# A spectral mixing layer and a feed-forward layer on one core: the first filter piece cast with its neighbours, and the work around it moved

## The chip, the cores and the metric

The kernel runs on one core of a Trainium2 chip. The time is the device time of one execution in microseconds, and lower is better. Times within the profiled execution are counted from the start of its span. PE is TensorE (matrix products, with PEld for its weight loads), DVE is VectorE, ACT is ScalarE, POOL is GpSimd, SP is SyncE. SP and POOL issue the DMAs here: SP's go over a hardware queue, POOL's over a software queue, and only POOL's cast or accumulate on the way.

## What is computed

The input `x` holds 8 images of 3008 rows and 256 channels. Each image is filtered in the frequency domain, and the rows then pass through two matrix products with a PReLU between them.

```python
X = np.fft.rfft(x, axis=1)                        # x: 8 x 3008 x 256
F = (filt_r + 1j * filt_i)[None, :, :]            # 1505 x 256
y = np.fft.irfft(X * F, n=3008, axis=1)
h = y.reshape(24064, 256) @ w_in                  # 256 x 2048
g = np.maximum(h, 0.0) + alpha * np.minimum(h, 0.0)
out = g @ w_out                                   # 2048 x 256, float32
```

## The kernel before

The transform length is split as 3008 = 94 x 32, so that the transform of an image becomes small matrix products with constant tables: a first product over 94 points (`piece_a`), a turn of the axes, a second product over 32 points with the twiddle factors in the table `twf` (`piece_b`), the product with the filter, an inverse product with `twi` (`piece_c`), a turn back, and a last product over the 94 frequencies (`inverse`, called from `half_d` and `pair_d`), which writes `yT`, the filtered image with channels on the partitions. `yT` holds two images.

**Image 0** is handled by the class `First`, ahead of everything else (lines 359 to 449), with the turns done on PE through an identity matrix. Its second stage has 12 pieces `kp`. For each, `piece_b` makes a product on PE (L299), and DVE multiplies it with the filter into `uu` (L304). Then `piece_c` (L324) makes the inverse product into two banks `self.ops` and `keep_c` evicts them into `v`, two pieces at a time. The loop at lines 412 to 434 runs `piece_b` two pieces ahead of `piece_c`. `piece_c` takes its banks from the pool `psO`, which has two, for pieces 0 to 10, and from `psF`, which has one double bank, for piece 11. The pool `psH` has two double banks, written `hps`. `warm` (L376) issues products of the identity whose results nobody reads. After the loop, `half_t` turns `v` into `zt` (L346), and `half_d` makes the first quarter of `yT`.

The **filter** arrives in `filt_s`, cast to FP16 by POOL's DMAs in batches of pieces 1 to 3, 4 to 7 and 8 to 11, eight DMAs each (L122). Piece 0 is loaded by SP in FP32 into the tile `fst` and multiplied from there. `fst` has the tag `asb`, so it shares its buffer with `asb`, the first-product result of images 1 to 7. After the loop POOL copies `fst` into piece 0 of `filt_s` (L435), and then makes `filts_s`, the filter with its real and imaginary halves exchanged (L438, L440), for the later images.

The **tables** `twf`, `twi` and `twx` are loaded by SP in thirds (L365). A small DVE memset on the destination holds an SP or POOL DMA back until DVE has come that far: before the `fst` loads at i == 1, before the middle third of `twf` and the tables behind it at i == 3, before the later `twi` and `twx` thirds after `piece_b(0)`, and before the weights at kp == 4. ACT doubles each `twf` third into `twd` (`twice`). SP and POOL work through their DMAs in the order of the program, each waits for its own conditions, and whatever stands behind it waits too. The DMAs of a queue share eight semaphores in turn, so that one waits until the one eight places before it has landed.

**The matrix products** of the feed-forward layer run in 48 blocks of 512 (in places 384) rows. A block has 16 steps; in step j, `up(j)` makes the 128 hidden channels j with `w_in` (L485), ACT evicts two steps' worth into `gtb` (L494), DVE applies the slopes (L497, L499), and `down(j)` makes a sixteenth of the block before with `w_out` (L516). ACT evicts its result and SP stores it. `al_s` and `alm_s`, the slopes on the partitions, come from a PE transpose of `al16` (L447).

**Images 1 to 7** are worked on between those steps. `plan_fft` puts each piece at a step number, counted through all blocks; the order by engine is the order of the program, and nothing reorders it. For image 1, `piece_b` and its accumulating DMA `uu<-ww` on POOL (L191) stand at steps 36 to 66, `piece_c` (L210) at `c_at`, and the `pair_d` pieces at `d_at`, which write `yT` through the one `psF` bank; the second image's rows are first read at step 96. `x_at` are the steps at which POOL loads the next image's `xs`. Steps listed as `front` (those of `piece_a` and `piece_c`) run `down` ahead of the piece.

Of the kernel before, what the change touches and what calls it, by code (L numbers as in the profile page):

```python
# [10 lines left out]
FP32 = mybir.dt.float32  # L11
# [39 lines left out]
def kernel(  # L51
# [211 lines left out]
    class First(Fft):  # L263
        def __init__(self):
            super().__init__(0)
            self.at = p_fft.tile([128, NK, D], FP16, name="at")
            self.v = p_fft.tile([128, NK, D], FP16, name="v")
            self.zt = p_fft.tile([96, N2, D], FP16, name="zt")
            self.fst = p_fft.tile([128, 1, 2, D], FP32, name="fst", tag="asb")
            self.twd = gtb[:, 6:9].rearrange("p a b c -> p (a b c)").rearrange("p (k m) -> p k m", m=128)  # L270
            self.am = gtb[:, 0:6].rearrange("p a b c -> p (a b c)")
            self.vm = self.v.rearrange("p k d -> p (k d)")
# [20 lines left out]
        def piece_b(self, kp):  # L293
            hp = psH.tile([128, 2, 512], FP32, name="hps").rearrange("p r (i d) -> p r i d", i=2)
            for i in range(2):
                for par in range(2):
                    r = slice(64 * par, 64 * par + 64)
                    for e in range(2):
                        nc.tensor.matmul(hp[64 * e : 64 * e + 64, par, i],  # L299
                                         self.twd[r, 2 * kp + e, 64 * i : 64 * i + 64], self.at[r, 2 * kp + e],  # L300
                                         start=True, stop=True)
            uu = p_uw.tile([128, 2, 2, D], FP16, name="uu", bufs=3)
            fl = self.fst if kp < 1 else filt_s
            nc.vector.tensor_mul(uu, hp, fl[:, kp].unsqueeze(2).to_broadcast([128, 2, 2, D]))  # L304
            self.uw[kp] = uu

        def piece_c(self, kp):
            if kp % 2 == 0:
                self.ops = [psO.tile([128, 2, D], FP32, name="op") for _ in range(2)]
            if kp == 11:  # L310
                pf = banks(False)
                warm(2, pf[:, 0])
                self.ops = [pf[:, e].rearrange("p (k d) -> p k d", k=2) for e in range(2)]
            kb = 0 if kp == 11 else kp % 2
            u = self.uw.pop(kp)
# [53 lines left out]
    tables(nc.sync, ("twf",), 0, 8)  # L369
    load_filt(nc.gpsimd, filt_s, 1, 4)  # L370
    load_filt(nc.gpsimd, filt_s, 4, 8)
    load_filt(nc.gpsimd, filt_s, 8, 12)

    def warm(n, pw):
# [5 lines left out]
    for i in range(8):  # L380
        f0.piece_a(i, both[i % 2], i % 3 < 2)
        if i % 2 == 1:
            warm((4, 4, 6, 3)[i // 2], bank("o"))
        if i == 1:
            nc.vector.memset(f0.fst[:, 0, :, 0:1], 0.0)
            load_filt(nc.sync, f0.fst, 0, 1)
        if i == 3:
            nc.vector.memset(twf_s[:, 8:16, 0:1], 0.0)
            tables(nc.sync, ("twf",), 8, 16)
            tables(nc.sync, ("twi", "twx"), 0, 8)  # L390
            tables(nc.sync, ("twf",), 16, 24)
        if i == 5:
            f0.twice(0, 8)
# [18 lines left out]
    for kp in range(12):  # L412
# [5 lines left out]
        elif kp % 2 == 1:  # L418
            f0.keep_c(kp - 1, (on_act, on_act))
            if kp < 7:  # L420
                f0.turn_at(kp + 5, 2, on_act)
        if kp == 4:
            nc.vector.memset(win_s[:, 0, 0:2], 0.0)
            for kt in range(2):
                nc.gpsimd.dma_start(out=win_s[:, kt], in_=moe_w_in[kt * 128 : (kt + 1) * 128])
            xc[(1, 0)] = load_x(1, 0)
            for q in range(2):
                nc.gpsimd.dma_start(
                    out=wout_s[:, 8 * q : 8 * q + 8],
                    in_=moe_w_out[1024 * q : 1024 * q + 1024].rearrange("(j p) d -> p j d", p=128))  # L430
            for c in range(1, 4):
                xc[(1, c)] = load_x(1, c)
        if 7 <= kp < 10:
            warm(2, banks(False)[:, 0])
    nc.gpsimd.dma_start(out=filt_s[:, 0:1], in_=f0.fst)  # L435
    for o in range(0, 128, 64):
# [7 lines left out]
    for i, evict, kind, fill in ((0, on_act, "h", 1), (2, on_dve, "o", 0), (1, on_act, "o", 1), (3, on_dve, "f", 0)):  # L444
        f0.half_d(i, evict, kind, fill)
    alp = bank("o")
    nc.tensor.transpose(alp[:, 0:16], al16, id32)  # L447
    nc.vector.tensor_copy(al_s, alp[:, 0:16])
    nc.vector.tensor_scalar(alm_s, al_s, 1.0, -1.0, OP.mult, OP.add)

# [79 lines left out]
    def plan_fft(b, a_at, ta, quarters, x_at, b_at, add, c_at, d_at):  # L530
# [99 lines left out]
```

## Time and profile before

| what | value |
| --- | --- |
| median of 3 runs | 785.22 us (784.51 to 788.92) |
| profiled execution | 786.87 us |
| its span | 784.8 us |
| PE busy | 768.7 us (98%) |
| DVE, ACT, POOL busy | 595.2, 587.3, 142.6 us |
| chain that ended last, by engine | PE 92%, DMA 3%, DVE 2%, ACT 2% |
| end of the last filter product of image 0 | 32.75 us |
| first product of the feed-forward layer | 39.33 us |

The profile is a table of all instructions of one execution. A row gives the start and the length in us, the engine, the line of the kernel, the operation with output and input, the count of merged instructions, and in brackets how long the engine had been idle before it and what the trace takes to have ended that idle time. The last is an inference; where several things are waited for, the trace names one of them. A row of a window gives a stretch of time, and for each engine its busy time and its instructions, then the granted PE clock as a share of full speed, the DMA share and the GB/s.

### The profile page before, as it was taken

Reading aid. Unit: us, or ns where it says so; the run is one execution under the profiler, and the core shown is the slowest. Engines: PE = TensorE matmul, PEld = TensorE weight load, DVE = VectorE, ACT = ScalarE, POOL = GpSimd, SP = SyncE. Lnnn points to the kernel's source line nnn. Section 1 sums busy time; section 2 is a strip of 40 time slices with the busy share of each in tenths; the row PEclk is TensorE's granted clock in tenths of the full one; section 3 lists DMA queues with packets and bytes.
Section 4 is the critical chain, followed back from the end, with each engine's and each line's share of the span. In section 5 each row is a group of like instructions: output and inputs, shape, how many; then the busy total and the mean of one; then the engine's idle time right before and its main releaser. Section 6 shows DMA issues by size and latency. Waiting matters only on the chain.

```text
span 784.8 us, 16091 instructions
## 1 busy us (share of the span) xinstructions
PE 768.7 (98%) x6349; PEld 511.6 (65%) x6349; DVE 595.2 (76%) x1117; ACT 587.3 (75%) x673; POOL 142.6 (18%) x271
## 2 busy tenths in 40 slices
PE   8889999999999999999999999999999999999998
PEld 4546656666666666766666666766666666766666
DVE  3757985788868888788877888688877888766664
ACT  4678778888778877798767887788876777677664
POOL 6510571122102220122201222010210122000000
PEclk9999999999999999999999999999999999999999
DMA  9996697757754657555593655734474233511111
GB/s 174 163 183 187 129 204 173 221 135 166 142 153 108 147 135 148 135 127 122 132 206 82 146 127 128 189 81 108 110 153 129 57 86 92 145 40 28 42 41 54
DMA packets 95515, 100.64 MB, mean 128 GB/s; under 512 B 11328, under 2 KB 83280, under 8 KB 95248
## 3 DMA queue, kind: packets, MB, share of 16 engines
q1 hardware_dynamic: 80800, 70.25, 34.3%
q0 software_dynamic: 14640, 29.38, 21.6%
q8 instruction: 49, 0.80, 0.4%
q14 instruction: 26, 0.21, 0.1%
HBM read 55.28 MB, written 46.66 MB: 130 GB/s over the span
## 4 chain that ended last, share of the span: by engine, by line
PE 92%; DMA 3%; DVE 2%; ACT 2%; issue 1%; POOL 0%; SPq 0%; ACTq 0%; DVEq 0%; POOLq 0%
PE hps L485 41%; PE op L516 41%; PE hps L155 3%; PE psF L232 3%; PE psF L179 2%; PE hps L210 1%; DMA uu<-ww 1%; DMA twf_s<-c_twf 1%; ACT v L255 1%; ACT gtb L494 1%; DMA xs<-in_x_dram 1%; PE psF L346 1%; DMA fst<-in_filt_r_dram 1%; DVE m L497 1%; PE op L324 0%
## 5 line engine op out<-in xcount | busy, mean ns | idle before, releaser
L494 ACT ACTIVATE gtb<-hps 128x1024 f16<-128x1024 f32 (+1 forms) x384 | 385.8, 1005 | 133.1 <-PE hps L485 132.2
L516 PE MATMUL op<-wout_s,gtb 128*128 128x256 f16 x3008 | 436.3, 273 | 0.1
L485 PE MATMUL hps<-yT,win_s 128*128 128x512 f16 (+1 forms) x1536 | 434.9, 375 | 1.2 <-ACT gtb L494 1.1
L516 PEld LDWEIGHTS <-gtb 128*128 128x128 f16 x3008 | 294.0, 98 | 168.9 <-issue 0.9
L497 DVE TENSOR_SCALAR m<-gtb,alm_s 128x512 f16<-128x512 f16 (+1 forms) x768 | 232.8, 346 | 152.5 <-ACT gtb L494 151.5
L499 DVE TENSOR_TENSOR gtb<-gtb,m 128x2048 f16<-128x2048 f16 (+1 forms) x192 | 231.0, 1203 | 10.1
L485 PEld LDWEIGHTS <-win_s 128*128 128x128 f16 x1536 | 142.8, 98 | 61.4 <-issue 15.2
L193 POOL DMA_DIRECT2D sw<-ww x144 | 71.0, 501 | 380.8 <-DVE ww L186 377.9
L255 ACT ACTIVATE asb<-hps 96x1024 f16<-96x1024 f32 x56 | 57.1, 1020 | 13.9 <-PE hps L155 12.0
L521 ACT ACTIVATE osb<-op 128x512 f32<-128x512 f32 (+1 forms) x97 | 56.2, 579 | 5.3 <-issue 2.8
L255 ACT ACTIVATE v<-hps 128x1024 f16<-128x1024 f32 x42 | 43.0, 1025 | 15.9 <-PE hps L210 15.9
L255 ACT ACTIVATE yT<-psF 128x752 f16<-128x752 f32 x59 | 47.0, 797 | 7.8 <-PE psF L232 7.7
L112 POOL DMA_DIRECT2D xs<-in_x_dram x64 | 37.3, 672 | 82.6 <-PE hps L155 74.3
L186 DVE TENSOR_TENSOR ww<-psF,filts_s 128x1024 f16<-128x1024 f32 x42 | 51.1, 1217 | 0.0
L187 DVE TENSOR_TENSOR uu<-psF,filt_s 128x1024 f16<-128x1024 f32 x42 | 51.0, 1214 | 0.0
L155 PE MATMUL hps<-xs,wf_s 94*96 94x512 f16 x112 | 33.9, 384 | 2.0 <-ACT asb L255 2.0
L232 PE MATMUL psF<-wi_s,zt 96*128 96x94 f16 x500 | 31.2, 205 | 0.2
L232 PEld LDWEIGHTS <-zt 96*128 96x128 f16 x512 | 28.6, 98 | 2.9 <-issue 0.6
L191 POOL DMA_DIRECT2D uu<-ww x24 | 19.4, 1198 | 31.7 <-DVE uu L187 28.5
L198 DVE TENSOR_TENSOR uu<-uu,sw 128x1024 f16<-128x1024 f16 x36 | 24.6, 683 | 0.0
L210 PE MATMUL hps<-uu,twi_s 64*64 64x256 f16 x336 | 16.8, 271 | 1.5 <-DMA uu<-ww 0.8
L179 PE MATMUL psF<-at,twf_s 64*64 64x256 f16 x336 | 17.3, 281 | 0.0
(68 smaller groups left out, 171.6 us busy)
## 6 DMA issues: line engine op xcount, KB each, us to landing
out_dram<-osb SPq DMA_DIRECT2D x160, 128.0 KB
a_dram<-asb SPq DMA_DIRECT2D x28, 384.0 KB
v_dram<-v SPq DMA_DIRECT2D x84, 128.0 KB
zt<-v_dram SPq DMA_DIRECT2D x28, 384.0 KB
sw<-ww POOLq DMA_DIRECT2D x144, 64.0 KB, 2.3
at<-a_dram SPq DMA_DIRECT2D x20, 384.0 KB
xs<-in_x_dram POOLq DMA_DIRECT2D x32, 192.0 KB, 4.6
xs<-in_x_dram POOLq DMA_DIRECT2D x32, 184.0 KB, 5.9
```

What stands on the lines that cost most here:

```text
L155: nc.tensor.matmul(ps[0:96, u], wf1_s, xs[:, o : o + 512], start=True, stop=True)
L186: nc.vector.tensor_mul(ww, px, fs)
L187: nc.vector.tensor_mul(uu, px, f)
L193: nc.gpsimd.dma_start(out=sw[o : o + 32], in_=ww[i : i + 32])
L232: nc.tensor.matmul(ps[:, m], self.zt[:, 8 * g + 4 * mh + m, dh * 128 : dh * 128 + 128], wi3_s, start=True, stop=True)
L255: nc.scalar.activation(o, i, AF.Copy)
L485: nc.tensor.matmul(self.hps[:, j % 2, 0:tn], win_s[:, kt, j * 128 : (j + 1) * 128], yT[:, kt, self.t0 : self.t0 + tn], start=(kt == 0), st ...
L494: nc.scalar.activation(g[:, 2 * i : 2 * i + 2], self.hps[:, :, 0:tn], AF.Copy)
L497: nc.vector.tensor_scalar(m[:, 2 * i + h], g[:, 2 * i + h], 0.0, a, OP.min, OP.mult)
L499: nc.vector.tensor_add(g, g, m)
L516: nc.tensor.matmul(self.op[:, si - s0], self.gts[k][:, 128 * si : 128 * si + 128], wout_s[:, k], start=(si == s0 and k == 0), stop=(si == ...
L521: nc.scalar.activation(osb[:, 0:m], self.op[:, 0:m], AF.Copy)
```

## The change

The tile `fst` goes. Piece 0 of the filter is cast by POOL in one batch with pieces 1 to 3, and its copy into `filt_s` and the memset for it go. The weights and the loads of image 1 stand directly behind the filter on POOL's queue, with no memset to hold them. The tables that were issued at i == 3 are issued at i == 5. Piece 10 of the inverse takes its two banks from `psF`, and piece 11 takes one from `psH` and one from `psO`; the two fill products ahead of piece 11 write to the `psH` bank. The transpose of the slopes moves from ahead of the blocks to step 1. In the plan, image 1's `piece_c` moves from steps 48 to 78 to steps 50 to 80, four of its `pair_d` pieces and one `xs` load move by one or two steps, and the first six of image 2's `piece_a` steps move two steps earlier.

```diff
-            self.fst = p_fft.tile([128, 1, 2, D], FP32, name="fst", tag="asb")
...
-            fl = self.fst if kp < 1 else filt_s
-            nc.vector.tensor_mul(uu, hp, fl[:, kp].unsqueeze(2).to_broadcast([128, 2, 2, D]))
+            nc.vector.tensor_mul(uu, hp, filt_s[:, kp].unsqueeze(2).to_broadcast([128, 2, 2, D]))
...
-            if kp % 2 == 0:
+            if kp % 2 == 0 and kp < 10:
                 self.ops = [psO.tile([128, 2, D], FP32, name="op") for _ in range(2)]
+            if kp == 10:
+                pf = banks(False)
+                self.ops = [pf[:, e].rearrange("p (k d) -> p k d", k=2) for e in range(2)]
             if kp == 11:
-                pf = banks(False)
-                warm(2, pf[:, 0])
-                self.ops = [pf[:, e].rearrange("p (k d) -> p k d", k=2) for e in range(2)]
-            kb = 0 if kp == 11 else kp % 2
+                pf = [bank(kind) for kind in ("h", "o")]
+                warm(2, pf[0])
+                self.ops = [t.rearrange("p (k d) -> p k d", k=2) for t in pf]
+            kb = 0 if kp > 9 else kp % 2
...
-    load_filt(nc.gpsimd, filt_s, 1, 4)
+    load_filt(nc.gpsimd, filt_s, 0, 4)
     load_filt(nc.gpsimd, filt_s, 4, 8)
     load_filt(nc.gpsimd, filt_s, 8, 12)
+
+    for kt in range(2):
+        nc.gpsimd.dma_start(out=win_s[:, kt], in_=moe_w_in[kt * 128 : (kt + 1) * 128])
+    xc[(1, 0)] = load_x(1, 0)
+    for q in range(2):
+        nc.gpsimd.dma_start(
+            out=wout_s[:, 8 * q : 8 * q + 8],
+            in_=moe_w_out[1024 * q : 1024 * q + 1024].rearrange("(j p) d -> p j d", p=128))
+    for c in range(1, 4):
+        xc[(1, c)] = load_x(1, c)
...
-        if i == 1:
-            nc.vector.memset(f0.fst[:, 0, :, 0:1], 0.0)
-            load_filt(nc.sync, f0.fst, 0, 1)
-        if i == 3:
+        if i == 5:
             nc.vector.memset(twf_s[:, 8:16, 0:1], 0.0)
             tables(nc.sync, ("twf",), 8, 16)
             tables(nc.sync, ("twi", "twx"), 0, 8)
             tables(nc.sync, ("twf",), 16, 24)
-        if i == 5:
             f0.twice(0, 8)
...
-        if kp == 4:
-            nc.vector.memset(win_s[:, 0, 0:2], 0.0)
-            for kt in range(2):
-                nc.gpsimd.dma_start(out=win_s[:, kt], in_=moe_w_in[kt * 128 : (kt + 1) * 128])
-            xc[(1, 0)] = load_x(1, 0)
...
-            for c in range(1, 4):
-                xc[(1, c)] = load_x(1, c)
...
-    nc.gpsimd.dma_start(out=filt_s[:, 0:1], in_=f0.fst)
...
-    alp = bank("o")
-    nc.tensor.transpose(alp[:, 0:16], al16, id32)
-    nc.vector.tensor_copy(al_s, alp[:, 0:16])
-    nc.vector.tensor_scalar(alm_s, al_s, 1.0, -1.0, OP.mult, OP.add)
...
+    def slopes():
+        alp = bank("o")
+        nc.tensor.transpose(alp[:, 0:16], al16, id32)
+        nc.vector.tensor_copy(al_s, alp[:, 0:16])
+        nc.vector.tensor_scalar(alm_s, al_s, 1.0, -1.0, OP.mult, OP.add)
+
+    put(1, slopes)
...
-    plan_fft(1, range(12, 28, 2), 28, 4, (32, 40, 50, 58), range(36, 72, 6), 0, range(48, 84, 6),
-             (92, 94, 97, 100, 111, 121, 142, 154))
-    plan_fft(2, (50, 56, 62, 68, 74, 80, 82, 84), 90, 4, (57, 69, 81, 89),
+    plan_fft(1, range(12, 28, 2), 28, 4, (32, 40, 50, 56), range(36, 72, 6), 0, range(50, 86, 6),
+             (94, 95, 98, 101, 111, 121, 142, 154))
+    plan_fft(2, (48, 54, 60, 66, 72, 78, 82, 84), 90, 4, (57, 69, 81, 89),
```

More of the change, by code (lines that the diff above doesn't have):

```diff
@@ L421 @@
                 f0.turn_at(kp + 5, 2, on_act)
-        if kp == 4:
-            nc.vector.memset(win_s[:, 0, 0:2], 0.0)
-            for kt in range(2):
-                nc.gpsimd.dma_start(out=win_s[:, kt], in_=moe_w_in[kt * 128 : (kt + 1) * 128])
-            xc[(1, 0)] = load_x(1, 0)
[L427 to L430, printed above, removed]
-            for c in range(1, 4):
-                xc[(1, c)] = load_x(1, c)
         if 7 <= kp < 10:
             warm(2, banks(False)[:, 0])
-    nc.gpsimd.dma_start(out=filt_s[:, 0:1], in_=f0.fst)
     for o in range(0, 128, 64):
```

## The prediction

> **What bounds the kernel now.** The page first: over the whole span TensorE has little left to give back.
>
> ```profile
> span 784.8 us, 16091 instructions
> ...
> PE 768.7 (98%) x6349; PEld 511.6 (65%) x6349; DVE 595.2 (76%) x1117; ACT 587.3 (75%) x673; POOL 142.6 (18%) x271
> ```
>
> 768.7 of 784.8 us are PE time, so a gain can only come out of the 16.1 us in which PE is idle, or out of time in which its clock was cut. I then cut the span into stretches of 8 us: PE is fully busy in nearly all from 56 us on, and the idle time lies before 56 us and between 112 and 120 us. Those are also places the change touches. The windows around 50 us (time, then PE, PEld, DVE, ACT and POOL busy, granted clock, DMA):
>
> ```profile
> 48.00:52.00 4.00, 1.69 (x8) 0.70 (x7) 3.11 (x8) 2.69 (x4) 1.95 (x4) 1.00 0.48 95
> ...
> 52.60:56.10 3.50, 3.50 (x13) 1.65 (x12) 1.84 (x3) 2.04 (x2) 0.00 (x0) 0.51 0.99 239
> ...
> 56.10:60.00 3.90, 3.90 (x32) 3.04 (x31) 1.83 (x3) 3.03 (x3) 0.74 (x2) 1.00 0.98 250
> ```
>
> PE works only 1.69 of 4 us between 48 and 52, and right after it the granted clock is about half for 3.4 us, though PE never pauses there. The timeline says what stopped it:
>
> ```profile
> 40.83 0.57 POOL L435 DMA_DIRECT2D filt_s<-fst  x1 [2.11 <-DMA wout_s<-in_moe_w_out_dram]
> ...
> 48.42 1.13 DVE L497 TENSOR_SCALAR m<-gtb,alm_s 128x512 f16<-128x512 f16 x4
> ...
> 49.71 1.02 ACT L255 ACTIVATE asb<-hps 96x1024 f16<-96x1024 f32 x1 [1.31 <-DVE m L497]
> ...
> 49.84 1.95 POOL L438 DMA_DIRECT2D filts_s<-filt_s  x4 [8.44 <-DMA filt_s<-fst]
> ...
> 50.78 0.59 PE L155 MATMUL hps<-xs,wf_s 94*96 94x512 f16 x2 [1.99 <-ACT asb L255]
> ```
>
> ACT stands still for 1.31 us before the first `asb` eviction. The trace puts that down to DVE, but that DVE line starts at 48.42 and goes on working; what ends at the same moment is the copy `filt_s<-fst`: POOL, which waits for it to land, goes on at 49.84. `fst` and `asb` share one buffer, so the eviction cannot write before the copy has read. The second `asb` matrix product then waits 1.99 us for ACT. For the start I read the chain and then DVE's and PE's rows:
>
> ```profile
> 10.50 4.34 DMA fst<-in_filt_r_dram
> ...
> 14.86 6.48 DMA twf_s<-c_twf
> ...
> 21.36 1.06 ACT gtb L255
> ```
>
> ```profile
> 22.52 1.22 DVE L304 TENSOR_TENSOR uu<-hps,filt_s 128x1024 f16<-128x1024 f32 x1 [1.21 <-DMA filt_s<-in_filt_r_dram]
> ```
>
> ```profile
> 28.13 4.62 DVE L304 TENSOR_TENSOR uu<-hps,filt_s 128x1024 f16<-128x1024 f32 x4 [0.30 <-DMA filt_s<-in_filt_i_dram]
> ...
> 32.95 0.19 PE L324 MATMUL op<-twi_s,uu 64*128 64x64 f16 x1 [0.30 <-ACT v L255]
> ...
> 34.67 0.43 DVE L258 CAST v<-psF 128x256 f16<-128x256 f32 x1 [1.93 <-ACT v L255]
> ...
> 35.15 0.93 PE L346 MATMUL op<-id,v 128*96 128x128 f16 x8
> ```
>
> The eight `fst` loads on SP's queue stand ahead of the tables, the third table piece lands late, ACT waits for it (21.36). But the first-transform stage is tied to DVE's twelve filter products (L304, 1.22 us each): the fifth waited 1.21 us and the ninth 0.30 us for filter pieces, and the last four run back to back from 28.13 to 32.75. From that end to the first L346 it takes 2.40 us: piece 10 had waited for ACT to empty the `op` banks, so piece 11 stood behind it and two fill products. Last, the chain around 116 us:
>
> ```profile
> 107.98 1.64 POOL uu L191 x2
> ...
> 109.61 8.12 DMA uu<-ww
> ...
> 117.77 0.41 PE hps L210 x6
> ```
>
> Piece 4 of image 1's inverse waits for its accumulating DMA: PE idles 1.53 us in the stretch 112 to 120.
>
> **The change part by part.**
>
> *No `fst`: the wait at 48.42.* One FP32 tile goes, with eight SP issues (0.42 each), one DVE memset (0.06), one POOL copy (0.57) and its landing (8.7 us). `asb` then has no earlier user, and its eviction can start when ACT is free at 48.40: 1.31 us. Next late there is TensorE's wait for the two `hps` banks: the second L155 would start at 49.47, up 14 and 15 at 50.38 instead of 51.69, so the 1.31 goes through whole. POOL's filter copies (L438) start about 9 us earlier; no engine waited for them.
>
> *The clock.* With 1.3 us less idle PE is busy for some 2.4 of any 3.4 us there. The stretch 20 to 24, where PE was busy 1.57 of 4 us, kept clock 1.00, so what is left should not cut it. Half speed for 3.4 us is 1.7 us of PE work, but ACT would become the one waited for at step 16 (gtb until 53.83, PE ready at 53.43): I follow it to the product of step 18 and get 1.24. Between 0 (another cut falls elsewhere, or this one stays) and 1.7; I take 1.24. [...]
>
> *First filter piece on POOL's queue.* Eight DMAs grow from 48 to 64 KB; eight of 32 KB leave SP's queue. So 128 KB more of FP16 go over the software queue and 256 KB less over the hardware one. The first product (16.67) now needs the first batch. That batch had landed by 17.83, when the second product started with no filter wait; a third more of it, on a queue freed of `fst`, puts it at 17.2 to 17.9: 0.5 to 1.2 late. Four products of 1.22 then end at 22.1 to 22.8, against 22.52, where the fifth started after its 1.21 wait: hidden. What sets the end is the last batch (28.13). The same source rows are read either way and fewer bytes written, so I take 0; bounds: 0.3 earlier (DVE is free at 27.83) to 1.2 later (the first batch's delay handed through in full).
>
> *Tables at i==5.* SP waits for DVE's third cast (ends 12.69) instead of the second, but no longer for `fst` landings: it issued the four tables from 13.48 to 15.25 and now does from about 12.8. The last lands 6.48 us after issue at worst, about 20.5 instead of 21.34; ACT doubles it up to 1 us earlier and evicts pieces 0 and 1 earlier. Next late is the fifth product's filter: no gain at the end. The later tables wait for the first product and go 0.5 to 1.2 later; first use of the next at 25.34. I take 0.
>
> *Pieces 10 and 11.* With banks `psF`, `h` and `o`, piece 10 need not wait for ACT (32.95) and both fill products run before product 11 is there. From DVE's end at 32.75: piece 11 0.4 with its latency 0.1, then ACT 0.38 and DVE 0.43, perhaps one after the other as now, some waiting of 0.2: 1.55 instead of 2.40. Gain 0.85; bounds 0.3 (the fill products still in the way) and 1.3 (evictions side by side).
>
> *Weights right behind the filter.* DVE's memset (0.06) and POOL's wait for it (2.60) go; 24.4 instead of 27.00. `win_s` landed at most 8.9 us after issue, and its first use at 39.24 did not wait: 0. They are now queued ahead of nothing that moved except the image-1 loads, equally early, and of the copies L438, where no engine waits.
>
> *Slopes at step 1.* L447's 0.23 us on PE stood in a gap that DVE's `yT` eviction ends (L346 waits 0.38 for it); at step 1 PE waits for ACT's evictions (0.39 at 43.49). DVE's 0.16 and 0.17 end well before 41.50. 0, at worst 0.23 lost.
>
> *The plan of images 1 and 2.* Inverse pieces move two steps later (about 2 us at 1.05 us a step), the `xs` loads ahead of the accumulating DMA go one or two steps earlier: the 1.53 goes. But `pair_d` 0 and 1 stand at steps 94 and 95 instead of 92 and 94, with one `psF`: now 138.10 (PE) and evicted by 139.43, so the second could start at 139.43 instead of 139.20, ends 139.76, is evicted by about 140.8, and the block that reads it would be ready at 140.6: 0.2 + 0.3 lost. Net 1.0; bounds 0 (wait stays half, losses double) and 1.53.
>
> **Sum.** 1.31 + 1.24 + 0.85 + 0 + 1.0 = 4.4 us. The profiled execution took 786.87 (span 784.8 and 2.07 around it) and goes to 782.5. It stands 1.65 above the median of the runs, 785.22; with the same gain the median goes to 780.8, which I round to 781.0. Half a per cent is 3.9 us, about what a measurement of this kernel can tell from no change.
>
> **Rivals.**
>
> *The clock cut is not regained* (or it was in the profiled execution and not in the median one): 4.4 - 1.24 = 3.2, so 782.1, and with a last filter batch 1.2 late 783.3. For it: before's three runs lie 784.51 to 788.92, so something varies from run to run. Against: the cut follows directly on the idle stretch.
>
> *The stall is only replaced.* The claim that `fst` holds `asb` rests on two times that coincide and on the shared buffer. If ACT waited for DVE, as the trace has it, 1.31 and 1.24 stay: gain 1.85, 783.4. Against it: DVE runs through 49.71 without a break.
>
> *Slower: the weights push back the last tables.* `twi` and `twx` 16 to 24 are issued at 19 to 21 us, piece 8 needs them at 29.8. The 6.48 us that one 128 KB table took while filters streamed shows the hardware queue giving way. If they landed only after both `wout_s` halves (issue 26.5 to 27.5, 13.6 to land: 41), piece 8 would be 11 us late: 785.2 + 11 - 4.4 = 792. It decides from 29.8 + 4.4 + 3.9 = 38 us on. Against: the software queue holds filters until about 26, five us after the tables' issue. [...]
>
> **How the numbers follow.** All terms near their middle (gain above 3.9): 0.56. One of the first two rivals, or several terms at their low ends: 0.37 (782 to 785). The third, and things unseen of its sort: 0.07. So faster 0.56, same 0.37, slower 0.07. Upper ends of all terms: 1.31 + 1.7 + 1.3 + 0.3 + 1.53 = 6.1, 779.1; lower ends 1.31 + 0 + 0.3 - 1.2 - 0.23 + 0 = 0.2, 785.0. The range 778.5 to 785.0 holds both, with 0.6 below for what varies from run to run; the likeliest case alone 779.1 to 781.3.
>
> **What would show it.** Right: no idle ACT before the first `asb` eviction, granted clock 1.00 through 45 to 60, the last filter product's end to the first L346 under 1.8 us, no wait of L210 for `uu<-ww`, a short wait at steps 95 and 96. Wrong: a half-clock stretch elsewhere before 60, the ninth filter product later than 29.3, or piece 8 waiting for a table.

## The result

Over ten executions of each, run side by side, the kernel after took 782.68 us in the median (781.36 to 783.51) and the kernel before 785.31 (782.50 to 788.92). The ratio is 0.9963, with a 95% interval of 0.9945 to 0.9980. So the kernel is 0.37% faster: some 2.6 us, and not the 4.2 that the forecast of 781.0 gave against 785.22. The time lies in the range (778.5 to 785.0), but outside the likeliest case's own range (779.1 to 781.3). It fell into the case "same", which had 0.37.

The two profiled executions stand further apart than the medians: 786.87 and 782.69. From the page of the kernel after:

```profile
span 780.8 us, 16065 instructions
...
PE 767.5 (98%) x6349; PEld 509.7 (65%) x6349; DVE 595.5 (76%) x1115; ACT 586.9 (75%) x673; POOL 142.4 (18%) x270
```

TensorE idles 13.3 us instead of 16.1, and needs 1.2 us less for the same 6349 products. The windows at the place of the old stall (time, then PE, PEld, DVE, ACT and POOL busy, granted clock, DMA) and the timeline of the kernel after:

```profile
48.00:52.00 4.00, 3.38 (x19) 1.71 (x18) 2.84 (x6) 3.50 (x4) 0.49 (x1) 1.00 0.93 225
52.60:56.10 3.50, 3.50 (x27) 2.50 (x26) 2.20 (x5) 2.49 (x3) 1.53 (x3) 1.00 0.85 183
```

```profile
46.72 1.02 ACT L255 ACTIVATE asb<-hps 96x1024 f16<-96x1024 f32 x1
...
47.62 1.03 ACT L485 ACTIVATE gtb<-hps 128x1024 f16<-128x1024 f32 x1
47.79 0.59 PE L155 MATMUL hps<-xs,wf_s 94*96 94x512 f16 x2 [0.57 <-ACT asb L255]
```

No idle time stands before the first `asb` eviction any more, the second L155 waits 0.57 us instead of 1.99, and the clock is 1.00 throughout. The start, by DVE's rows and then PE's:

```profile
16.44 2.37 DVE L302 TENSOR_TENSOR uu<-hps,filt_s 128x1024 f16<-128x1024 f32 x2 [0.54 <-DMA filt_s<-in_filt_r_dram]
...
18.73 7.14 DVE L302 TENSOR_TENSOR uu<-hps,filt_s 128x1024 f16<-128x1024 f32 x6
27.47 4.62 DVE L302 TENSOR_TENSOR uu<-hps,filt_s 128x1024 f16<-128x1024 f32 x4 [1.61 <-DMA filt_s<-in_filt_i_dram]
```

```profile
32.64 0.38 ACT L255 ACTIVATE v<-hps 128x256 f16<-128x256 f32 x1 [0.21 <-PE op L325]
32.67 0.42 DVE L258 CAST v<-op 128x256 f16<-128x256 f32 x1 [0.58 <-PE op L325]
...
33.41 0.85 PE L347 MATMUL op<-id,v 128*96 128x128 f16 x8
```

The first eight filter products run with hardly a gap; only the ninth waits, 1.61 us, for the last filter batch. The two evictions of piece 11 go side by side (32.64 and 32.67), so from the last filter product's end (32.09) to the first turn product it is 1.32 us where it was 2.40. Last, the place of the wait at 116 us, as the window of the same 8 us, and the list of what PE waits for from 60 to 160 us in the kernel after (us in total, times, longest):

```profile
112.00:120.00 8.00, 7.97 (x59) 5.00 (x57) 4.82 (x10) 6.92 (x8) 2.53 (x5) 1.00 0.92 179
```

```profile
PE psF L232 <- DMA zt<-v_dram: 0.4, 1, 0.4
PE hps L476 <- ACT gtb L485: 0.2, 1, 0.2
```

L210's wait for `uu<-ww` is gone; a short one of `pair_d` for `zt` has come.

Where the time went is read best from the starts of the products that open the steps (L485 before, L476 after), in the two profiled executions:

| Stretch | before, us | after, us | change |
|---|---|---|---|
| start to step 0 | 39.33 | 37.50 | -1.83 |
| steps 0 to 12 | 8.43 | 8.70 | +0.27 |
| steps 12 to 18 (old stall and half clock) | 9.51 | 6.89 | -2.62 |
| steps 18 to 40 | 24.26 | 24.26 | 0.00 |
| steps 40 to 66 | 28.59 | 29.54 | +0.95 |
| steps 66 to 90 (old wait of L210) | 24.60 | 22.83 | -1.77 |
| steps 90 to 106 (`pair_d`) | 14.74 | 15.69 | +0.95 |
| step 106 to the end | 635.35 | 635.35 | 0.00 |

The sum is -4.05, the difference of the spans. Two stretches that the prediction had at nothing got longer, and a third by more than was priced.

### The profile page after: what moved, and what is told of

It is laid out like the page before. It is cut to its first block, busy times and chain, and to the rows that moved or that the text cites. A ratio compares the mean times of both kernels' runs of the same rounds, so it can differ in the third digit from the quotient of the medians.

```text
span 780.8 us, 16065 instructions
## 1 busy us (share of the span) xinstructions
PE 767.5 (98%) x6349; PEld 509.7 (65%) x6349; DVE 595.5 (76%) x1115; ACT 586.9 (75%) x673; POOL 142.4 (18%) x270
## 4 chain that ended last, share of the span: by engine, by line
PE 93%; DMA 3%; ACT 1%; POOL 1%; DVE 1%; issue 0%; ACTq 0%; DVEq 0%; POOLq 0%
PE hps L476 42%; PE op L507 41%; PE hps L155 3%; PE psF L232 3%; PE psF L179 2%; PE hps L210 1%; DMA xs<-in_x_dram 1%; ACT gtb L485 1%; DMA filt_s<-in_filt_r_dram 1%; DMA zt<-v_dram 1%; DMA filt_s<-in_filt_i_dram 1%; PE psF L347 1%; POOL filt_s L122 1%; POOL xs L112 0%; PE hps L387 0%
## 5 line engine op out<-in xcount | busy, mean ns | idle before, releaser
L485 ACT ACTIVATE gtb<-hps 128x1024 f16<-128x1024 f32 (+1 forms) x384 | 385.8, 1005 | 132.4 <-PE hps L476 131.6
L476 PE MATMUL hps<-yT,win_s 128*128 128x512 f16 (+1 forms) x1536 | 434.2, 375 | 1.6 <-ACT gtb L485 1.4
L476 PEld LDWEIGHTS <-win_s 128*128 128x128 f16 x1536 | 142.7, 98 | 60.9 <-issue 14.5
L255 ACT ACTIVATE v<-hps 128x1024 f16<-128x1024 f32 (+1 forms) x43 | 43.4, 1009 | 13.6 <-PE hps L210 13.2
L155 PE MATMUL hps<-xs,wf_s 94*96 94x512 f16 x112 | 33.6, 381 | 0.6 <-ACT asb L255 0.6
L232 PE MATMUL psF<-wi_s,zt 96*128 96x94 f16 x500 | 31.2, 205 | 0.7 <-DMA zt<-v_dram 0.4
L232 PEld LDWEIGHTS <-zt 96*128 96x128 f16 x512 | 28.5, 98 | 3.8 <-issue 0.9
L179 PE MATMUL psF<-at,twf_s 64*64 64x256 f16 x336 | 17.3, 281 | 0.0
L210 PE MATMUL hps<-uu,twi_s 64*64 64x256 f16 x336 | 16.6, 272 | 0.0
```

Of the source, the lines that this page charges most:

```text
L155: nc.tensor.matmul(ps[0:96, u], wf1_s, xs[:, o : o + 512], start=True, stop=True)
L232: nc.tensor.matmul(ps[:, m], self.zt[:, 8 * g + 4 * mh + m, dh * 128 : dh * 128 + 128], wi3_s, start=True, stop=True)
L255: nc.scalar.activation(o, i, AF.Copy)
L476: nc.tensor.matmul(self.hps[:, j % 2, 0:tn], win_s[:, kt, j * 128 : (j + 1) * 128], yT[:, kt, self.t0 : self.t0 + tn], start=(kt == 0), st ...
L485: nc.scalar.activation(g[:, 2 * i : 2 * i + 2], self.hps[:, :, 0:tn], AF.Copy)
```

## The experiments

All were run in twelve executions each, in three groups (experiments 1, 2, 4 and 5; then 3, 6, 7 and 8; then 9 to 12), each group beside 35 executions of the kernel before: 784.99, 785.25 and 784.97 us in the median. Each ratio below is against the kernel before of its own group; only the third group holds the kernel after as well (experiment 10), so that other differences from the kernel after are across groups. An interval of a ratio is about 0.0015 wide to either side, 1.2 us: a single part of this change is smaller than that in most cases, so the medians stand beside stretches of the traces, which are steadier. "With a cut clock" counts the executions whose mean granted clock lies under 0.9985, wherever in the execution the cut falls; a cut of 3.4 us at half speed makes 0.998.

**1. The copy alone.** The kernel before, with one line moved: `filt_s<-fst` is issued ahead of the weights instead of behind them.

```diff
         if kp == 4:
+            nc.gpsimd.dma_start(out=filt_s[:, 0:1], in_=f0.fst)
             nc.vector.memset(win_s[:, 0, 0:2], 0.0)
...
-    nc.gpsimd.dma_start(out=filt_s[:, 0:1], in_=f0.fst)
```

> The kernel before, with one thing moved: POOL issues the copy filt_s<-fst ahead of the weights instead of behind image 1's loads, so it lands near 35 us and fst gives its buffer up long before step 12. Theory (fst holds asb): ACT's 1.31 us idle before the first asb eviction is gone, PE's gap at 49 shrinks by as much, no half-clock stretch follows, and step 18 starts about 2.5 us earlier than in the kernel before (57.27 -> 54.7); the time falls by 1.3 (stall alone) to 2.6 us. Rival (ACT waited for DVE, as the trace names it): the idle time stays 1.3 us and the time stays where it was.

782.32 us (781.28 to 785.15), ratio 0.9964 [0.9949, 0.9979]; one of twelve executions with a cut clock. The timeline and a window of this kernel:

```profile
48.14 1.02 ACT L255 ACTIVATE asb<-hps 96x1024 f16<-96x1024 f32 x1
...
49.21 0.38 PE L155 MATMUL hps<-xs,wf_s 94*96 94x512 f16 x1 [0.57 <-ACT asb L255]
```

```profile
50.00:54.00 4.00, 3.58 (x22) 2.14 (x22) 2.87 (x6) 3.48 (x5) 0.49 (x1) 1.00 0.93 199
```

Nothing but the copy's place differs from the kernel before, and ACT's idle time ahead of `asb` is gone with PE's long wait. So it was the copy that held `asb`, and not DVE, which the trace named. Steps 12 to 18 take 6.89 us, as in the kernel after. And one moved line brings 2.7 us, as much as the whole change.

**2. The stall without the cut.** The kernel before, with eight fill products of the sort that the kernel has at its start put at step 14, in the gap. They compute nothing that is used.

```diff
+    put(14, lambda: warm(8, bank("o")))
```

> The kernel before, with eight fill products (0.22 us each) put on PE at step 14, inside its idle time behind the asb wait; the wait itself stays. Theory (the idle time cuts the clock, and the cut costs of its own): ACT still idles 1.3 us before asb, PE is busy through the gap, the granted clock stays 1.00 from 45 to 60, and step 18 comes 1.2 us earlier than in the kernel before; the median falls by 0.8 to 1.3 us, since not every execution need have had the cut, and the runs spread less than the 6 us of the kernel before. Rival (the cut costs nothing, since ACT is waited for anyway, or has another cause): step 18 and the median as before within 0.3 us.

783.80 us (782.58 to 784.65), ratio 0.9984 [0.9970, 0.9998]; two of twelve with a cut clock. Its timeline and two windows:

```profile
47.95 1.02 ACT L255 ACTIVATE asb<-hps 96x1024 f16<-96x1024 f32 x1 [1.16 <-DVE m L497]
...
48.09 0.50 POOL L438 DMA_DIRECT2D filts_s<-filt_s  x1 [8.82 <-DMA filt_s<-fst]
```

```profile
48.00:52.00 4.00, 3.40 (x17) 1.55 (x15) 1.83 (x3) 3.74 (x5) 1.95 (x4) 1.00 0.82 166
50.00:54.00 4.00, 3.70 (x23) 2.26 (x23) 2.38 (x5) 3.48 (x4) 0.04 (x1) 1.00 1.00 230
```

The stall is left (1.16 us ahead of `asb`, and POOL still waiting for the copy), but PE is busy and the clock stays whole. Steps 12 to 18 take 8.17 us. That splits the gain at this place: 9.51 - 8.17 = 1.34 for the cut, 8.17 - 6.89 = 1.28 for the stall. (Against the other profiled execution of the kernel before, in experiment 3, where these steps take 9.30 us, the cut is 1.13.) The medians say much the same: 1.2 from the kernel before to this one, 1.5 from this one to experiment 1.

**3. The kernel before once more**, as an experiment of its own, to see how often the cut comes and where.

> The kernel before once more, for the granted clock and the span of each of its executions and for a second profile. [...]

785.09 us (783.82 to 787.52), ratio 0.9996 [0.9976, 1.0016]; eight of twelve with a cut clock. The windows of its profiled execution:

```profile
20.00:24.00 4.00, 3.68 (x78) 2.37 (x77) 2.13 (x2) 2.94 (x4) 2.55 (x5) 0.64 1.13 226
...
48.00:52.00 4.00, 1.93 (x8) 0.79 (x8) 3.36 (x8) 2.93 (x4) 1.95 (x4) 0.98 0.52 104
52.00:55.20 3.20, 3.20 (x11) 1.47 (x9) 0.92 (x4) 1.65 (x3) 0.00 (x0) 0.50 0.77 177
```

The cut at 52 us is there again, and before it one in the filter stage (from 21.11 us on), where the clock was 1.00 in the execution that the prediction was made from. Of the 105 executions of the kernel before in the three groups, 63 have a cut clock, with a median of 785.57; the other 42 have 783.80. Of the 22 executions of the kernel after (ten, and twelve in experiment 10), three have one. So cuts, at whatever place, cost 785.04 - 783.80 = 1.24 us in the median of all 105.

Where a cut falls can be read from these traces. In the kernel before the clock is at 0.50 for 3.413 us, from 52.67 to 56.09, and at 1.00 ahead of it and behind it. The two cuts of this execution start at 21.11 and 51.83 us, 30.72 apart, which is nine times 3.413. That stretches of this length follow on one another through an execution is my estimate from this one pair. By it I counted back from each cut, 3.413 us at a time, and took PE's busy time in each stretch:

| Execution | stretch of 3.413 us | PE busy, us | clock in the next 3.41 us |
|---|---|---|---|
| experiment 3 | 17.70 to 21.11 | 1.55 | 0.50 |
| experiment 3 | 48.42 to 51.83 | 1.34 | 0.50 |
| kernel before | 18.54 to 21.95 | 2.28 | 1.00 |
| kernel before | 21.95 to 25.36 | 2.11 | 1.00 |
| kernel before | 49.26 to 52.67 | 1.57 | 0.50 |
| experiment 9 | 20.70 to 24.11 | 1.54 | 0.50 |

In the kernel before, the gap of the filter stage (PE busy 1.01 us from 20.00 to 23.40) lies, so counted, across two stretches (busy 2.28 and 2.11) and was not cut; in experiment 3 a gap of the same stage falls into one (busy 1.55) and was. From 7 to 60 us no other stretch of these three executions has PE busy for less than 2.5 us, and none of the others is followed by a cut.

**4. The old plan in the kernel after.**

```diff
-    plan_fft(1, range(12, 28, 2), 28, 4, (32, 40, 50, 56), range(36, 72, 6), 0, range(50, 86, 6),
-             (94, 95, 98, 101, 111, 121, 142, 154))
-    plan_fft(2, (48, 54, 60, 66, 72, 78, 82, 84), 90, 4, (57, 69, 81, 89),
+    plan_fft(1, range(12, 28, 2), 28, 4, (32, 40, 50, 58), range(36, 72, 6), 0, range(48, 84, 6),
+             (92, 94, 97, 100, 111, 121, 142, 154))
+    plan_fft(2, (50, 56, 62, 68, 74, 80, 82, 84), 90, 4, (57, 69, 81, 89),
```

> The changed kernel with the step numbers of images 1 and 2 of the kernel before. By the prediction's term the plan is worth 1.0 us: span 781.8, with L210 waiting 1.5 us for uu<-ww near 112 us. By the trace of the changed kernel the gain of the later inverse pieces (0.8 us by step 90) is given back at steps 93 to 96 (0.9 us): span 780.6 to 781.0, steps 72 to 90 about 0.8 later and step 96 level.

781.88 us (780.00 to 784.23), ratio 0.9959 [0.9942, 0.9976]: no slower than with the new plan, 0.8 faster if anything. PE's waits in its trace show the wait back again, 0.8 us in total where it had 1.53 in the kernel before:

```profile
PE hps L210 <- DMA uu<-ww: 0.8, 2, 0.5
```

Every experiment but 6 has one of the two plans, so their traces can be put side by side; the kernel before and experiments 1 to 4 and 9 have the old one, the kernel after and experiments 5, 7, 8, 10 and 12 the new one. (Experiment 11, in whose execution a cut falls into this stretch, and 6, which has a plan of its own, are left out of the table.)

| Stretch | old plan, six traces, us | new plan, six traces, us | means |
|---|---|---|---|
| steps 40 to 66 | 28.59 to 29.19 | 29.54 to 29.55 | +0.67 |
| steps 66 to 90 | 22.80 to 25.30 | 22.82 to 22.83 | -1.43 |
| steps 90 to 106 | 14.74 to 14.85 | 15.09 to 15.72 | +0.73 |
| steps 106 to 128 | 21.88 | 21.88 | 0.00 |

The new plan does take the wait away, in all six traces; it gives the same amount back ahead of it and behind it. (Three of the old-plan traces stand at 29.1 to 29.2 in the first stretch, since L210 already waits at step 66 there; the other three at 28.6.) What the first stretch loses is no wait: PE is busy 29.47 of its 29.54 us in the kernel after, and 28.52 of 28.59 in the kernel before. Pieces b (L179) and c (L210) of image 1 stood at the same step in the old plan, and stand two steps apart in the new one. The kernel after, by its timeline:

```profile
86.25 0.41 PE L179 MATMUL psF<-at,twf_s 64*64 64x256 f16 x8
...
86.59 0.63 PE L155 MATMUL hps<-xs,wf_s 94*96 94x512 f16 x2
...
88.89 0.41 PE L210 MATMUL hps<-uu,twi_s 64*64 64x256 f16 x8
...
89.30 0.38 PE L476 MATMUL hps<-yT,win_s 128*128 128x512 f16 x1
```

and the kernel before:

```profile
90.43 0.41 PE L179 MATMUL psF<-at,twf_s 64*64 64x256 f16 x8
...
90.67 0.39 PE L210 MATMUL hps<-uu,twi_s 64*64 64x256 f16 x8
...
91.00 0.82 PE L485 MATMUL hps<-yT,win_s 128*128 128x512 f16 x3
```

Next to each other the two groups of 64-row products overlap and take 0.57 us (90.43 to 91.00); apart they take 0.34 (86.25 to 86.59) and 0.41 (88.89 to 89.30), 0.75 together, each counted up to the start of the next product. Four such pairs (steps 48, 54, 60 and 66) lie in or at the edge of the stretch. Step by step, the whole of the 0.95 us lies at these four: 0.16 around step 48 and some 0.25 around each of the others, while the rest is the same within 0.03. At steps 72 and 78 the same two moves, of `piece_c` and of image 2's `piece_a`, were made where no `piece_b` stands beside them. Steps 71 to 74 and 77 to 80 take 4.01 and 3.92 us in the kernel after, and 4.03 and 3.93 in experiment 2, which has the old plan and no wait there: nothing lost.

**5. The old accumulators of pieces 10 and 11 in the kernel after.**

```diff
-            if kp % 2 == 0 and kp < 10:
+            if kp % 2 == 0:
                 self.ops = [psO.tile([128, 2, D], FP32, name="op") for _ in range(2)]
-            if kp == 10:
+            if kp == 11:
                 pf = banks(False)
+                warm(2, pf[:, 0])
                 self.ops = [pf[:, e].rearrange("p (k d) -> p k d", k=2) for e in range(2)]
...
-            kb = 0 if kp > 9 else kp % 2
+            kb = 0 if kp == 11 else kp % 2
```

> The changed kernel with the accumulators of pieces 10 and 11 as in the kernel before. Theory (0.85 us): from the end of the last filter product to the first product of the turn 2.4 us instead of 1.5, and the feed-forward layer starts 0.9 us later; span 781.7. Rival (the gain at that place came from the filter landing earlier, or is taken back by ACT's chain behind it): step 14 within 0.3 us of the changed kernel's 48.70.

783.35 us (782.18 to 785.62), ratio 0.9981 [0.9967, 0.9995], so 0.67 above the kernel after. Its timeline:

```profile
32.06 0.19 PE L322 MATMUL op<-twi_s,uu 64*128 64x64 f16 x1 [0.30 <-ACT v L255]
...
33.79 0.42 DVE L258 CAST v<-psF 128x256 f16<-128x256 f32 x1 [1.53 <-ACT v L255]
34.27 0.34 PEld L344 LDWEIGHTS <-v 128*96 128x96 f16 x3 [0.46 <-DVE v L258]
34.27 0.48 PE L344 MATMUL op<-id,v 128*96 128x128 f16 x3
```

Piece 10 waits for ACT again, and the evictions go one behind the other. From the last filter product's end (31.05 + 1.22 = 32.27) to the first turn product it is 2.00 us, against 1.32, and from there to step 0 4.18 against 4.09: 0.77 together, near what the medians have.

**6. The old plan, with the two late pieces of image 1 one step later.** This was to keep four b and c pieces together and yet give the last two the time that the accumulating DMA needs. The slopes are at their old place here too.

```diff
-    plan_fft(1, range(12, 28, 2), 28, 4, (32, 40, 50, 56), range(36, 72, 6), 0, range(50, 86, 6),
-             (94, 95, 98, 101, 111, 121, 142, 154))
-    plan_fft(2, (48, 54, 60, 66, 72, 78, 82, 84), 90, 4, (57, 69, 81, 89),
+    plan_fft(1, range(12, 28, 2), 28, 4, (32, 40, 50, 56), range(36, 72, 6), 0, (48, 54, 60, 66, 73, 79),
+             (92, 94, 97, 100, 111, 121, 142, 154))
+    plan_fft(2, (50, 56, 62, 68, 74, 80, 82, 84), 90, 4, (57, 69, 81, 89),
```

> The changed kernel with two parts put otherwise: image 1's inverse pieces at steps 48, 54, 60, 66, 73 and 79 with the other plan steps as in the kernel before (xs load at 56 as in the changed one), and the slopes turned ahead of the blocks again. Theory (a second-stage piece and an inverse piece at one step share the array and take 0.57 us instead of 0.75 apart; the wait for uu<-ww goes with one step of delay alone; slopes at step 1 cost 0.2 to 0.3): steps 0 to 12 take 8.4 us instead of 8.7, steps 40 to 100 take 60.5 to 61.0 instead of 61.9, steps 100 to 128 0.3 less; the median is 1.5 to 2 us below the changed kernel's. Rival (the plan is worth nothing either way): 40 to 100 between 61.5 and 62.

784.49 us (782.40 to 785.86), ratio 0.9986 [0.9970, 1.0002]: a miss, 1.8 slower than the kernel after. PE's waits in its trace:

```profile
PE psF L232 <- DMA zt<-v_dram: 1.7, 1, 1.7
```

The pairs did bring what they should: steps 40 to 66 take 28.60 us, as in the old plan, 0.95 less than in the new one. But the last c piece is one step later and `pair_d` is where it was, and the way through DRAM that makes `zt` isn't done in time: the wait that went from L210 comes back at L232. (Experiment 11, with both at their old places, shows such a wait too, so the one step is likely but not shown as its cause.) Steps 66 to 80 also took 16.31 us, against 14.46 in the kernel after and 16.27 in the kernel before with its wait. PE idles 1.12 us of them, against 0.03 in the kernel after, and is busy 0.76 longer, all around steps 72 to 74 and 78 to 80, where the c piece stands one step ahead of a `piece_a` of image 2; why that costs so much isn't settled.

**7, 8 and 12. The loads of the start, put back one at a time.** In experiment 7 it is piece 0 of the filter: `fst` on SP's queue again, with the tables at i == 3, and its copy ahead of the last pieces as in experiment 1. The weights stay right behind the filter.

```diff
+            fl = self.fst if kp < 1 else filt_s
...
-    load_filt(nc.gpsimd, filt_s, 0, 4)
+    load_filt(nc.gpsimd, filt_s, 1, 4)
...
+        if i == 1:
+            nc.vector.memset(f0.fst[:, 0, :, 0:1], 0.0)
+            load_filt(nc.sync, f0.fst, 0, 1)
+        if i == 3:
...
+        if kp == 4:
+            nc.gpsimd.dma_start(out=filt_s[:, 0:1], in_=f0.fst)
```

> The changed kernel with piece 0 of the filter in FP32 on SP's queue again, as in the kernel before, its tables at i==3, and the copy into filt_s issued at kp == 4, early enough that asb does not wait. Theory (the first piece's place is worth nothing at the end, the range was 0.3 gained to 1.2 lost): the last filter product ends within 1 us of the changed kernel's 32.1, and the median is within 0.5 us. Rival (the SP loads delay the last filter batch): the last product ends near 33 and the median is 0.6 to 1 us above the changed kernel's.

784.09 us (782.15 to 785.52), ratio 0.9985 [0.9968, 1.0002]; five of twelve with a cut clock, and 783.93 in the median of the other seven. This too is a miss: 1.4 above the kernel after, more than the rival's 0.6 to 1, and without its sign, since the last filter product ended at 31.63 in the profiled execution and not near 33. Experiment 1 has the same `fst` on the same queue and took 782.32. Beside the plan, the banks and the slopes, the two differ in that the weights are held back until the fourth piece there. The profiled execution took 782.42 and shows a start like that of the kernel after (step 0 at 37.48), so the trace does not tell where the others lose.

The weights and the loads of image 1 held until the fourth piece, as before, in the kernel after (experiment 8; the lines go back into `kp == 4` with their memset):

```diff
+        if kp == 4:
+            nc.vector.memset(win_s[:, 0, 0:2], 0.0)
+            for kt in range(2):
+                nc.gpsimd.dma_start(out=win_s[:, kt], in_=moe_w_in[kt * 128 : (kt + 1) * 128])
+            xc[(1, 0)] = load_x(1, 0)
```

> The changed kernel with the weights and image 1's loads held back to kp == 4 by the DVE memset, as in the kernel before. Theory (hidden): POOL issues them about 3 to 4 us later and nobody waits, the median within 0.4 us of the changed kernel's. Rival (held weights leave the queue to the tables and the last filter batch): the ninth filter product starts up to 1 us earlier and the median falls by as much.

782.07 us (781.50 to 784.20), ratio 0.9962 [0.9944, 0.9979]. The tables at i == 3 in the kernel after (experiment 12):

```diff
-        if i == 5:
+        if i == 3:
             nc.vector.memset(twf_s[:, 8:16, 0:1], 0.0)
...
+        if i == 5:
             f0.twice(0, 8)
```

> The changed kernel with the tables issued at i==3, as before. The prediction took 0 for this. Theory (the tables are not what the end waits for): the last filter product ends within 0.7 us of the changed kernel's and the median within 0.4 us. Rival (tables issued two casts earlier take the transfers' time from the filter): the fifth or ninth product waits longer and the median rises by 0.5 us or more, which would put part of what the first piece's place is worth here.

782.56 us (781.47 to 784.75), ratio 0.9966 [0.9950, 0.9982]. Neither place is worth anything that can be measured. The start is seen better in the traces: the last filter product ends between 31.2 and 32.9 us in the four executions of kernels whose start is that of the kernel before (the kernel before, experiments 1, 2 and 3; mean 32.34), and between 31.1 and 33.1 in the nine that have all the filter on POOL's queue (mean 32.23). That is 0.1 us between the kinds and up to 2 us between executions of one kind: the 0.65 us that the kernel after won at this place in the pair of profiles is well within chance.

**9 and 11. The start alone**, that is, the kernel after with the old plan and the slopes at their old place (experiment 9), and the same with the weights held (experiment 11). Their edits are the plan of experiment 4, the weights of experiment 8 (11 only), and for the slopes:

```diff
+    alp = bank("o")
+    nc.tensor.transpose(alp[:, 0:16], al16, id32)
+    nc.vector.tensor_copy(al_s, alp[:, 0:16])
+    nc.vector.tensor_scalar(alm_s, al_s, 1.0, -1.0, OP.mult, OP.add)
...
-    put(1, slopes)
```

> The changed kernel with two of its parts undone: the plan of images 1 and 2 and the place of the slopes are those of the kernel before. Theory (the plan costs 0.4 to 0.8 us in the middle and 0.3 behind step 100, the slopes 0.2 to 0.3 in steps 0 to 12): steps 0 to 12 take 8.43 us, steps 40 to 128 0.3 to 1.0 less than in the changed kernel, and the median is 0.6 to 1.2 us below the changed kernel's in the same call. Rival (both parts are worth what they cost): within 0.3 us of it.

> As the run with the old plan and the old place of the slopes, and with the weights held back to kp == 4 as well, so that of the change there stay the first filter piece, the tables at i==5 and the banks of pieces 10 and 11. Theory (the weights' place is worth nothing): the median within 0.4 us of that run's. Rival (held weights free the queue for the last filter batch): 0.5 us or more below it.

782.04 us (780.68 to 784.58), ratio 0.9959 [0.9944, 0.9974], and 781.49 (780.34 to 787.31), ratio 0.9970 [0.9950, 0.9990]. The first is 0.7 below the kernel after in its group (experiment 10), within the 0.6 to 1.2 that was expected, but the intervals overlap. The second is the lowest median of all, and not outside the noise of the kernel after either. Its one outlier is the profiled execution; PE's waits there:

```profile
PE psF L232 <- DMA zt<-v_dram: 2.8, 1, 2.8
```

Behind that wait the clock was at half for 6.83 us, twice 3.413 (mean granted clock 0.995). With the slopes at their old place, steps 0 to 12 take 8.43 us in both; in all traces with the slopes at step 1 they take 8.69 to 8.70.

**10. The kernel after once more**, in the same group as experiments 9, 11 and 12.

> The changed kernel once more, beside the others of this call and for a second profile. Expected: a median of 782.4 to 783.0, the lower clock in at most three executions of twelve, steps 0 to 12 in 8.7 us, 12 to 18 in 6.9 us, 40 to 100 in 61.9 us again, since no wait in those stretches hangs on a transfer that varies; only the start differs.

782.77 us (781.18 to 786.07), ratio 0.9985 [0.9970, 1.0000]; one of twelve with a cut clock. The median agrees with that of the first ten executions, 782.68.

## Why the prediction was right in its sign and too high in its size

The terms of the sum, against what the runs showed for each:

| Term | Predicted, us | Shown, us | By |
|---|---|---|---|
| no `fst`: the wait at 48.42 | 1.31 | 1.28 | experiments 1 and 2 |
| the clock | 1.24 | 1.13 and 1.34 in two executions that have the cut; 1.2 between the medians | experiments 2 and 3 |
| pieces 10 and 11 | 0.85 | 0.77 (experiment 5), 1.17 between the profiles | experiment 5 |
| first piece, tables, weights | 0 | 0.1, between starts that differ by up to 2 | the thirteen traces, experiments 8 and 12 |
| slopes | 0 | -0.27 | experiments 9 and 11 |
| the plan | 1.0 | 0.0 | experiment 4 |

**The stall** was read rightly, with its cause: the trace put the wait down to DVE, and the reading by the shared buffer held (experiment 1). The rival "the stall is only replaced" falls with it.

**The clock** came out at the size of the step, and the rival that it is not regained falls: three of 22 executions of the kernel after have a cut, against 63 of 105. That the medians have the size of one cut in one execution is in part luck, since four executions in ten have no cut and others, like the profiled one of experiment 3, have two. The step's working had a weak place, though it did no harm: that the stretch 20 to 24 us kept its clock with PE busy 1.57 of 4 us was taken as a sign that such a gap isn't cut. There the gap lay across two stretches of 3.413 us (busy 2.28 and 2.11), and in another execution the same stage was cut, with a stretch busy 1.55; only the three executions in the table of experiment 3 show this, and where the stretches lie in them is an estimate. What the traces show of the length: the cuts of experiment 3 start nine times 3.413 us apart, and every cut ahead of an execution's last products lasts 3.413 us or, in experiment 11, twice that. What they show of the gap: PE was busy 1.34 to 1.57 of the 3.41 us ahead of each cut in the table, and filling the gap (experiment 2, 3.40 of 4 us) kept the clock.

**Pieces 10 and 11** went as the step says, with evictions side by side rather than one behind the other, at least in seven of the nine traces that have the new banks (1.32 to 1.37 us from the last filter product to the first turn product); in experiments 7 and 9 it took 1.76 and 1.75.

**The first piece, the tables and the weights** are worth nothing that could be seen, as the step had it and for its reason: the end of the stage is set by the last filter batch (27.47, the only one with a long wait). The rival in which the weights push back the last tables did not come. Nor does the 6.48 us of one table show a queue that gives way: in the trace of the kernel before the 64 KB filter DMAs of the software queue that were issued around it (from 14.41 to 16.89 us) took 5.5 to 6.7 us to land, against 3.5 to 4.8 for those issued from 20.95 us on. The first eight products even ran earlier than before, which only made the ninth wait 1.61 us instead of 0.30.

**The slopes** cost a little more than the step named as the worst: 0.27 in steps 0 to 12, by experiments 9 and 11 (8.43) against the kernel after (8.70). Nothing comes back ahead of step 0: from the first turn product to step 0 it is 4.09 us in these two as well. "0, at worst 0.23 lost" should have taken the latter: at the old place PE stood idle anyway, and at step 1 the product adds to the steps, whatever waits are near.

**The plan** is the step that failed. "The 1.53 goes" is right: -1.43 in the mean of six traces against six. "0.2 + 0.3 lost" at `pair_d` was too little, 0.73 in the mean: 0.35 in experiment 10, where nothing waits for `zt`, and up to 0.98 where `pair_d` 0 waits for it by up to 0.5 us. The rest of the miss was not in the sum at all: the c pieces were moved away from the b pieces beside which they overlapped, and the step counted only what a move does to waits, not what it does to the instructions' neighbours. That cost 0.95 of busy time against an execution of the old plan with no wait in that stretch. The prediction's opening, by which only idle time and a cut clock have anything to give, leaves no room for such a term: how long PE is busy with the same products depends on which stand side by side. Experiment 6 paired the four again and got the 0.95 back. Image 2's a pieces moved back with them there, but at steps 72 and 78 the same moves without a b piece beside them cost nothing, so it is what stands beside the b pieces that costs: a c piece before, an a piece after. The rows of one pair (0.57 against 0.75) give 0.72 for four; the last 0.2 isn't explained.

**From the profiled execution to the median.** The sum was made against one execution, and there it nearly came: -4.18 for 4.4. That was in part luck: 0.65 us of it is where the last filter product ended, and pieces 10 and 11 gave 1.17 there where experiment 5 has 0.77. (The plan had no part in it: steps 40 to 90 took 53.19 us in that execution, and 53.13 in the mean of the six with the old plan.) "With the same gain the median goes to 780.8" was a step that couldn't be made without knowing which of these the median execution has too. By the terms as shown the gain between medians should be 1.28 + 1.2 + 0.77 + 0.1 - 0.27 + 0 = 3.1. Measured are 2.6 and, in the later group, 2.2 between the medians (1.2 by the ratio of 0.9985, which is not the quotient of the medians). The differences are within the intervals; no further cause was looked for.

What stays open: why experiment 7 is slower than experiment 1 and the kernel after, and the 16.3 us of steps 66 to 80 in experiment 6. Also, the three fastest versions (experiments 4, 9 and 11: 781.88, 782.04 and 781.49) have the old plan in common, but experiment 8 with the new one stands right behind them (782.07), and their intervals overlap with that of the kernel after, so that they are faster isn't shown.

## What to carry to other kernels

Where a change has many parts, look first for one that ends a stall with a cut clock behind it (here PE busy 1.57 of 3.41 us, then clock 0.50 for 3.41 us): the one moved line, the copy that frees a shared buffer, gave 2.7 us, and all the rest together nothing that could be measured. When a piece is moved in a schedule to end a wait, price its neighbours too: what did it overlap with at the old place, and what is due right behind it at the new one? And before a wait of one profiled execution is put into the sum, see whether it depends on when a DMA lands, since such waits may be half as long in the next execution (1.53 and 0.8 us here). The same holds for the clock: one trace in which a gap was followed by full speed does not show that the gap is harmless.

## What was not expected of the hardware

- In four places of three executions, 3.413 us in which PE was still busy 1.34 to 1.57 us (39 to 46%) were followed by half clock for the next 3.413 us. A gap of the kernel before with PE busy 1.01 us from 20.00 to 23.40, across two stretches by the estimate in experiment 3 (busy 2.28 and 2.11), was not. It isn't the same in every execution of one program: 63 of 105 show a cut clock, and by the traces the cuts began at 52.67 us in one execution of the kernel before, at 21.11 and 51.83 in another, and at 24.11 in experiment 9.
- Two groups of eight products of 64 rows, of two pieces of one image and in different banks, take 0.57 us next to each other and 0.75 apart.
- The start, which the loads feed, ends up to 2 us earlier or later from one execution to another of kernels that are the same up to there: the last filter product ended between 31.1 us (experiment 4) and 33.1 (experiment 10), and over the fourteen traces the first one started between 16.3 and 17.9.
